# A recorded and re-ordered attention + FFN kernel: another transfer model and instruction pages in its planner, 10 warming matmuls for 20

## The chip, the cores and the metric

One core of a Trainium2 chip. The metric is device time of one execution in microseconds (us). Engines: PE (TensorE matmul), PEld (its weight loads), DVE (VectorE), ACT (ScalarE), SP (SyncE, which issues all the transfers here).

## The reference

```python
# attention: 4 batches, 8 heads, 512 local + 32 global tokens, head size 64
s_g  = scale * q_g @ k_all.T ; out_g = sm(s_g) @ v_all          # global queries see all keys
s_ll = where(|i - j| <= 32, scale * q_l @ k_l.T, -1e9)          # local queries: a band
s_l  = concat([scale * q_l @ k_g.T, s_ll]) ; out_l = sm(s_l) @ concat([v_g, v_l])
x    = concat([out_g, out_l])                                   # 2176 rows of 512
# first FFN, 1536 wide
g = x @ w_gate ; x = (g / (1 + exp(-g)) * (x @ w_val)) @ w_out
# second FFN, 2048 wide
h = x @ w_in ; out = (max(h, 0) + alpha * min(h, 0)) @ w_out2
```

All data is float32. The weights come as pairs of words of 64 bits that the kernel converts; products are made in three passes of high and low halves.

## The kernel before, in words

The kernel has two parts. The first part (attention of all batches, the first FFN of batches 0 to 2, and the preparation of the second FFN's weights) is not issued as the Python code runs: a `Planner` records each operation of PE, DVE, ACT and SP as an atom with its reads, writes and a cost (`record`, `price`). `flush` then asks `order` for a sequence and issues the operations in it; each engine works through its own list strictly in order. `order` simulates the four engines: each engine has a time at which it is free, an atom is ready when its predecessors are done, and of the atoms that are ready within `LOOK` (0.1 us) the one with the earliest due time is taken. Due times come from the recorded order of the matmuls. Transfers have one common time, `dma`, to which each adds bytes / `DMA`. All instructions of the recorded part carry line L272 in the profile. The second part (from `nc.flush()` on, L1199 and later lines) is issued as written.

The head of the recorded part is the attention of batch 0: four pairs of heads, u0 to u3. For each: `mm` (scores: 32 products of 128 columns, each two matmul records in the profile, so 64), `soft` (DVE mask and maximum, ACT exp), `t` (4 transposes and a copy `pt`), `pv` (64 records), `to` (4 transposes, then `xa` as high and low half). Ahead of it `heat(HEAT)` issues matmuls on a zero tile. Then `visit1` runs the first FFN: per block f of 128 hidden columns 12 matmuls for g, 12 for v, 12 for the output product, with `sg` (ACT), `t` (DVE), and `h` as high and low half (ACT, then DVE) between. The attention of the next batch and the weight conversion are spread between these blocks. A conversion: a load into a `dbl` or `yp` buffer, two ACT steps, three DVE steps (`raw`, `dbl`, `raw`), then split into high and low halves (`w`), and a store for the second use.

From the second batch on `w2_prepare` converts the second FFN's weights in the same way: load to `dbl`, convert, store `w2sx`, `w2so` from `dbl`, and for sums `w2ss` in two halves, one from `raw` and one from a scratch in the tail of `xa` (`out_to`, L869 to L882). `xa` holds x.T of a batch, high and low halves. At the change to the unrecorded part, `third` (L1182) lays four operands (t3, t1, b21, t4) over all of `xa`.

Of the kernel before, what the change touches and what calls it, by code (L numbers as in the profile page):

```python
# [10 lines left out]
F32 = mybir.dt.float32  # L11
# [13 lines left out]
N3 = 320  # L25
# [6 lines left out]
GWIN = (1, 4, 13, 15, 7, 10)  # L32
NG = len(GWIN)
P = dict(
    SLACK=60.0, LOOK=0.1, SWITCH=4.0, MARGIN=0.5, HEAT=20, ND=3, NR=3, LAG=6,
    wr0=0.75, wr2=0.5, wr3=0.75, wr4=0.6, wr5=0.2,
    ns1=33, ns2=34, ns3=32, g1=1.0, g2=1.1, g3=1.0,
    lo0=0.0, lo1=0.0, lo2=0.0, lo3=0.0, hi0=0.0, hi1=0.25, hi2=0.25, hi3=0.5,
# [13 lines left out]


class Op:
    __slots__ = ("eng", "op", "args", "kw", "reads", "writes", "cost", "lat", "table")


class Planner:
# [6 lines left out]


    ENGINES = ("tensor", "vector", "scalar", "sync")
    TABLE, DMA, START, LAST = 1.28, 405.0, 0.75, 10.0

    def __init__(self, tc):  # L70
        self.tc, self.nc = tc, tc.nc
# [51 lines left out]
    @staticmethod  # L123
    def price(o, outs, ins):
        n = int(np.prod(outs[0].shape[1:]))
        psum = any("PSUM" in str(a.space) for a in ins)
        o.lat = 0.14
        if o.eng == "tensor":
            o.lat = 0.23
            if o.op == "transpose":  # L130
                o.cost = n * 2 / 2400 + 0.003
            elif ins[0].dtype == F32R:
                o.cost = n / 2400 + 0.0133
            elif ins[0].dtype == BF16:
                o.cost = n / 2400 + 0.007
            elif n == 128:
                o.cost = 0.037
            else:
                o.cost = n * 4 / 2400 / 4 + 0.008
        elif o.eng == "vector":  # L140
            two = o.op in ("tensor_scalar", "tensor_copy") and not psum and ins[0].dtype == F32
            o.cost = n / (1920 if two else 960) + 0.075 + (n * 7 / 960 if o.op == "reciprocal" else 0)
        elif o.eng == "scalar":
            o.lat = 0.16
            wide = ins[0].ap[-1][0] > 1 or ins[0].dtype == U32
            o.cost = n / 1200 + 0.075 + (0.2 if o.kw.get("accum_out") is not None else 0) + (0.12 if wide else 0)
            f = o.kw.get("func")
            o.table = None if f == ACTF.Copy else f
        else:
            o.cost = 0.45  # L150
            a = outs[0]
            o.lat = int(np.prod(a.shape)) * mybir.dt.size(a.dtype) / 1e3 / Planner.DMA
# [27 lines left out]
    def order(self):  # L180
# [20 lines left out]
                d = min(d, due[j] - size[i] - atoms[i][-1].lat)  # L201
            due[i] = d
        free = {e: self.START for e in self.ENGINES}
        table, dma = None, 0.0
        left = [len(b) for b in before]
        done = [None] * N
        ready = {e: {} for e in self.ENGINES}
# [18 lines left out]
        while len(plan) < N:  # L226
# [19 lines left out]
            done[i] = []  # L246
            y = x
            if e == "sync":
                y += 0.45
                dma = max(dma, y + 1.0) + atoms[i][0].lat  # L250
                done[i] = [dma + 0.9]
            else:
                for o in atoms[i]:
                    y += o.cost
                    done[i].append(y + o.lat)
            free[e] = y
# [65 lines left out]
def kernel(  # L322
# [44 lines left out]

    ident = const.tile([128, 128], F32, name="ident")
    ex = Slots(const, {"y30": (1, 1024), "y31": (1, 1024)})
    xa = const.tile([128, 2, 4, 640], F32R, name="xa")  # L370
    yp = [const.tile([128, 2, 4, 256], F32, name=f"yp{b}") for b in range(B - 1)]
    y3 = {}

# [487 lines left out]
    def w2_prepare():  # L861
# [6 lines left out]
        def out_to(key, raw):  # L868
            w2s[key] = dram.tile([128, 2, 1024], F32, name="w2s%s%d" % key)  # L869
            if key[0] != "s" or not nc.recording:  # L870
                t = dbl.bitcast(F32R).rearrange("p (h c) -> p h c", h=2)
                yield from split(t, raw)
                nc.sync.dma_start(out=w2s[key], in_=t.bitcast(F32))
                return
            hi, lo = xa.rearrange("p h k c -> p (h k) c")[:, :, S:640], raw.rearrange("p (k c) -> p k c", c=128)
            st["tail"] = True
            nc.scalar.activation(out=hi, in_=lo, func=ACTF.Copy)
            yield
            nc.vector.tensor_tensor(out=lo.bitcast(F32R), in0=lo, in1=hi, op=ALU.subtract)
            nc.sync.dma_start(out=w2s[key][:, 0].rearrange("p (k c) -> p k c", c=128), in_=hi.bitcast(F32))  # L880
            nc.sync.dma_start(out=w2s[key][:, 1], in_=raw)
            st["tail"] = False  # L882

# [152 lines left out]
    if True:  # L1036
# [145 lines left out]
        def third():  # L1182

            while wq:
                wload(True)
            while st.get("tail"):
                next(w2gen)
            flat = xa.rearrange("p h k c -> p (h k c)")
            for i, name in enumerate(("t3", "t1", "b21", "t4")):
                ops1[name] = oper(flat[:, 4 * N3 * i:4 * N3 * i + 4 * N3], N3)  # L1190
            x_split(2, ops1["b11"], (0, 0))
            for name in ("t2", "t3", "t1"):
                x_split(2, ops1[name], sums[name])
            x_split(2, ops1["b21"], (1, 0))
            x_split(2, ops1["t4"], sums["t4"])
# [182 lines left out]
        x_split(0, ops["t1"], t1)  # L1378
        t4 = next(sums)[1]
        x_split(0, ops["t3"], next(sums)[1])  # L1380
        flat = xa.rearrange("p h k c -> p (h k c)")
        for i, name in enumerate(("b21", "t4", "b22")):
            ops[name] = oper(flat[:, 4 * NT * i:4 * NT * i + 4 * NT], NT)
        x_split(0, ops["b21"], (1, 0))
        x_split(0, ops["t4"], t4)
        x_split(0, ops["b22"], (1, 1))
# [194 lines left out]
```

## Time and profile before

| | |
|---|---|
| median of 3 runs | 897.06 us (897.03 to 897.11) |
| the profiled execution | 896.01 us |
| its span, first to last instruction | 894.2 us |
| mean granted clock of TensorE, as a share of full | 0.997 |
| PE busy | 866.7 us (97%) |
| DVE busy | 692.1 us (77%) |
| ACT busy | 528.2 us (59%) |

A row of a timeline gives the start in us, the time in us, engine, line, operation, output <- input with shapes, and the number of instructions merged; in brackets the engine's idle time before it and what ended it. "issue" stands for a wait for nothing that the profile shows. Matmul records overlap, since matmuls are pipelined. The tile a, g, v, acc stand for banks of PSUM.

### The profile page before, as it was taken

Reading aid. Unit: us, or ns where it says so; the run is one execution under the profiler, and the core shown is the slowest. Engines: PE = TensorE matmul, PEld = TensorE weight load, DVE = VectorE, ACT = ScalarE, POOL = GpSimd, SP = SyncE. Lnnn points to the kernel's source line nnn. Section 1 sums busy time; section 2 is a strip of 40 time slices with the busy share of each in tenths; the row PEclk is TensorE's granted clock in tenths of the full one; section 3 lists DMA queues with packets and bytes.
Section 4 is the critical chain, followed back from the end, with each engine's and each line's share of the span. In section 5 each row is a group of like instructions: output and inputs, shape, how many; then the busy total and the mean of one; then the engine's idle time right before and its main releaser. Section 6 shows DMA issues by size and latency. Waiting matters only on the chain.

```text
span 894.2 us, 17315 instructions
## 1 busy us (share of the span) xinstructions
PE 866.7 (97%) x6868; PEld 749.0 (84%) x6868; DVE 692.1 (77%) x1442; ACT 528.2 (59%) x1051; POOL 0.7 (0%) x6
## 2 busy tenths in 40 slices
PE   6799999999899999899999999999999999999997
PEld 5577778787688787778999999999999999989996
DVE  4997889969778865688666677777896777977776
ACT  5889999767667688554333346434555434554442
POOL 0000000000000000000000000000000000000000
PEclk9999999999999999999999999999999999999999
DMA  9899899798986789985656665546375554675731
GB/s 360 300 393 414 334 354 361 289 351 321 407 358 219 301 323 370 335 306 192 212 189 206 237 247 212 228 156 267 142 266 229 211 213 172 252 272 225 280 141 60
DMA packets 48833, 239.30 MB, mean 268 GB/s; under 512 B 4848, under 2 KB 13680, under 8 KB 26480
## 3 DMA queue, kind: packets, MB, share of 16 engines
q1 hardware_dynamic: 48752, 238.19, 70.8%
q8 instruction: 54, 0.88, 0.4%
q14 instruction: 27, 0.22, 0.1%
HBM read 183.38 MB, written 54.79 MB: 266 GB/s over the span
## 4 chain that ended last, share of the span: by engine, by line
PE 78%; DMA 10%; ACT 5%; DVE 5%; issue 1%; SPq 0%; ACTq 0%; DVEq 0%
PE ps_acc L1451 21%; PE ps_g L1239 9%; PE ps_v L1239 9%; PE ps_a L1239 8%; PE acc L272 8%; PE v L272 7%; PE g L272 7%; PE a L272 5%; PE ps_acc L1296 3%; DMA dbl<-in_w_dram 3%; DMA w2so<-dbl 2%; PE ps_a L1296 2%; DMA w2sx<-dbl 2%; DVE dbl L272 1%; DMA yp<-in_w_dram 1%
## 5 line engine op out<-in xcount | busy, mean ns | idle before, releaser
L1451 PE MATMUL ps_acc<-w,hring 128*128 128x512 f32 x816 | 194.2, 391 | 0.0
L1451 PEld LDWEIGHTS ps_acc<-w,hring 128*128 128x128 f32 x816 | 152.0, 188 | 30.1 <-ACT hring L1420 0.3
L272 PE MATMUL acc<-h,w 128*128 128x512 f32 x432 | 108.2, 399 | 3.1 <-ACT h L272 2.2
L272 PE MATMUL g<-xa,w 128*128 128x512 f32 x432 | 107.8, 398 | 2.5 <-ACT sg L272 1.6
L272 PE MATMUL v<-xa,w 128*128 128x512 f32 x432 | 107.1, 396 | 0.2 <-issue 0.2
L1415 ACT ACTIVATE r<-c 128x384 f32<-128x384 f32 (+1 forms) x96 | 47.8, 498 | 92.9 <-DVE c L1247 92.9
L272 PEld LDWEIGHTS acc<-h,w 128*128 128x128 f32 x432 | 81.0, 191 | 22.3 <-ACT h L272 2.5
L1456 DVE TENSOR_TENSOR oacc<-ps_acc,oacc 128x512 f32<-128x512 f32 x119 | 81.9, 691 | 22.2 <-PE ps_acc L1451 20.9
L272 PEld LDWEIGHTS g<-xa,w 128*128 128x128 f32 x432 | 78.9, 188 | 22.8 <-ACT sg L272 3.0
L272 PEld LDWEIGHTS v<-xa,w 128*128 128x128 f32 x432 | 79.3, 188 | 18.6 <-issue 1.8
L1420 ACT ACTIVATE hring<-g 128x384 fp32r<-128x384 f32 (+1 forms) x96 | 48.6, 506 | 55.9 <-DVE g L1417 55.6
L272 ACT ACTIVATE e<-e,mx 128x128 f32<-128x128 f32 (+1 forms) x136 | 57.2, 423 | 14.6 <-DVE mx L272 14.2
L1421 DVE TENSOR_TENSOR hring<-g,hring 128x384 fp32r<-128x384 f32 (+1 forms) x96 | 51.1, 532 | 18.9 <-ACT hring L1420 16.1
L1417 DVE SCALAR_TENSOR_TENSOR g<-g,nal,r 128x384 f32<-128x384 f32 (+1 forms) x96 | 56.8, 591 | 10.4 <-ACT g L1416 9.7
L272 ACT ACT_TABLE_LOAD x46 | 59.0, 1283 | 8.0 <-PE g L272 6.6
L1416 ACT ACTIVATE g<-c 128x384 f32<-128x384 f32 (+1 forms) x96 | 47.9, 499 | 13.9 <-DVE hring L1421 13.9
L1239 PE MATMUL ps_g<-xa,w 128*128 128x320 f32 (+1 forms) x288 | 53.3, 318 | 0.2
L1239 PE MATMUL ps_v<-xa,w 128*128 128x320 f32 (+1 forms) x288 | 53.2, 319 | 0.1
L1239 PE MATMUL ps_a<-w 128*128 128x384 f32 (+1 forms) x288 | 51.4, 326 | 0.0
L1239 PEld LDWEIGHTS ps_g<-xa,w 128*128 128x128 f32 x288 | 47.1, 188 | 1.9 <-ACT p L1255 0.4
L1239 PEld LDWEIGHTS ps_v<-xa,w 128*128 128x128 f32 x288 | 46.8, 188 | 1.6 <-DVE u L1263 0.4
L1239 PEld LDWEIGHTS ps_a<-w 128*128 128x128 f32 x288 | 47.9, 188 | 0.1
(211 smaller groups left out, 1397.7 us busy)
## 6 DMA issues: line engine op xcount, KB each, us to landing
dbl<-in_w_dram SPq DMA_DIRECT2D x28, 1024.0 KB, 8.0
w<-w2so SPq DMA_DIRECT2D x24, 1024.0 KB, 5.3
w<-w2sx SPq DMA_DIRECT2D x24, 1024.0 KB, 4.8
w<-w2ss SPq DMA_DIRECT2D x24, 1024.0 KB, 6.4
v<-in_v_dram SPq DMA_DIRECT2D x15, 1024.0 KB, 10.0
qk<-in_qk_dram SPq DMA_DIRECT2D x14, 688.0 KB, 9.5
w2sx<-dbl SPq DMA_DIRECT2D x8, 1024.0 KB, 8.0
w2so<-dbl SPq DMA_DIRECT2D x8, 1024.0 KB, 9.7
```

Of the source, the lines that this page charges most:

```text
L272: last[o.eng] = getattr(getattr(self.nc, o.eng), o.op)(*o.args, **o.kw)
L1239: nc.tensor.matmul(out=o[:, 0:n], lhsT=left(name, a, k), rhs=x[name][:, b, k, 0:n], start=(i == 0), stop=(i == 5),)
L1296: mm = nc.tensor.matmul(out=o, lhsT=a, rhs=x, start=(first and e == 0 and not second), stop=((j, f, e) == (NF1 // 2 - 1, 0, 2) and i not i ...
L1415: nc.scalar.activation(out=rr, in_=u, func=ACTF.Relu)
L1416: nc.scalar.activation(out=g, in_=u, func=ACTF.Relu, scale=-1.0)
L1417: nc.vector.scalar_tensor_tensor(out=g, in0=g, scalar=nal[:, i:i + 1], in1=rr, op0=ALU.mult, op1=ALU.add)
L1420: nc.scalar.activation(out=hi, in_=g, func=ACTF.Copy)
L1421: nc.vector.tensor_tensor(out=lo, in0=g, in1=hi, op=ALU.subtract)
L1451: nc.tensor.matmul(out=o, lhsT=a, rhs=x, start=(i == 0), stop=(i == 5))
L1456: nc.vector.tensor_tensor(out=oacc[tb], in0=o, in1=oacc[tb], op=ALU.add)
```

## The change

Four things. `HEAT` goes from 20 to 10. In the planner's simulation a transfer now starts 0.3 us after SP takes it up (before: 1.0 us after the 0.45 us of its issue), runs at 385 instead of 405 bytes per ns and is done 1.9 instead of 0.9 us after its last byte. PE's instructions are counted there (4 for a float32 matmul, 2 for others, 66 ahead of the first), and PE enters a page of 256 no sooner than 6.2 us after the page before. And `xa` becomes one flat tile: the first 4096 columns are x.T in rows of 512 (before: in rows of 640, of which the last 128 were the scratch), the last 1024 the scratch `tail`.

```diff
-    SLACK=60.0, LOOK=0.1, SWITCH=4.0, MARGIN=0.5, HEAT=20, ND=3, NR=3, LAG=6,
+    SLACK=60.0, LOOK=0.1, SWITCH=4.0, MARGIN=0.5, HEAT=10, ND=3, NR=3, LAG=6,
...
-    TABLE, DMA, START, LAST = 1.28, 405.0, 0.75, 10.0
+    TABLE, DMA, START, LAST, PAGE, FIRST, FETCH = 1.28, 385.0, 0.75, 10.0, 256, 66, 6.2
...
-        o.lat = 0.14
+        o.lat, o.words = 0.14, 0
         if o.eng == "tensor":
             o.lat = 0.23
+            o.words = 4 if o.op == "matmul" and ins[0].dtype == F32 else 2
...
-        table, dma = None, 0.0
+        table, dma, words, entered = None, 0.0, self.FIRST, [self.START]
...
             if e == "sync":
+                dma = max(dma, y + 0.3) + atoms[i][0].lat
+                done[i] = [dma + 1.9]
                 y += 0.45
-                dma = max(dma, y + 1.0) + atoms[i][0].lat
-                done[i] = [dma + 0.9]
             else:
                 for o in atoms[i]:
+                    words += o.words
+                    while words >= self.PAGE * len(entered):
+                        if len(entered) > 1:
+                            y = max(y, entered[-1] + self.FETCH)
+                        entered.append(y)
                     y += o.cost
                     done[i].append(y + o.lat)
...
-    xa = const.tile([128, 2, 4, 640], F32R, name="xa")
+    xall = const.tile([128, 16 * N3], F32R, name="xa")
+    xa = xall[:, 0:8 * S].rearrange("p (h k c) -> p h k c", h=2, k=4)
+    tail = xall[:, 8 * S:8 * S + 1024]
...
-            hi, lo = xa.rearrange("p h k c -> p (h k) c")[:, :, S:640], raw.rearrange("p (k c) -> p k c", c=128)
             st["tail"] = True
-            nc.scalar.activation(out=hi, in_=lo, func=ACTF.Copy)
+            nc.scalar.activation(out=tail, in_=raw, func=ACTF.Copy)
             yield
-            nc.vector.tensor_tensor(out=lo.bitcast(F32R), in0=lo, in1=hi, op=ALU.subtract)
-            nc.sync.dma_start(out=w2s[key][:, 0].rearrange("p (k c) -> p k c", c=128), in_=hi.bitcast(F32))
+            nc.vector.tensor_tensor(out=raw.bitcast(F32R), in0=raw, in1=tail, op=ALU.subtract)
+            nc.sync.dma_start(out=w2s[key][:, 0], in_=tail.bitcast(F32))
             nc.sync.dma_start(out=w2s[key][:, 1], in_=raw)
...
-                ops1[name] = oper(flat[:, 4 * N3 * i:4 * N3 * i + 4 * N3], N3)
+                ops1[name] = oper(xall[:, 4 * N3 * i:4 * N3 * i + 4 * N3], N3)
```

The last replacement stands in the same form once more, for the operands of the second FFN.

## Rows read from the trace of the kernel before

**Rows 1.** The page: busy time and instructions of each engine; the instruction queue.

```profile
PE 866.7 (97%) x6868; PEld 749.0 (84%) x6868; DVE 692.1 (77%) x1442; ACT 528.2 (59%) x1051; POOL 0.7 (0%) x6
...
q8 instruction: 54, 0.88, 0.4%
```

**Rows 2.** Busy time by stretch: length, engines, PEclk, DMA share, GB/s.

```profile
0.00:50.00 50.00, 36.16 (x698) 27.79 (x698) 33.81 (x112) 35.30 (x93) 0.70 (x6) 1.00 0.88 340
50.00:200.00 150.00, 149.00 (x1692) 118.24 (x1696) 129.24 (x298) 136.15 (x260) 0.00 (x0) 1.00 0.92 354
200.00:240.00 40.00, 35.04 (x304) 26.45 (x293) 36.94 (x80) 30.20 (x48) 0.00 (x0) 0.96 0.95 361
...
233.40:236.70 3.30, 3.30 (x8) 2.65 (x9) 3.27 (x6) 1.19 (x2) 0.00 (x0) 0.50 1.01 382
...
420.00:890.00 470.00, 469.39 (x2606) 433.77 (x2604) 360.32 (x688) 204.96 (x437) 0.00 (x0) 1.00 0.56 211
```

**Rows 3.** PE's smaller waits, 200 to 240 us: us in total, times, longest.

```profile
PE a L272 <- DVE o L272: 0.7, 1, 0.7
PE a L272 <- ACT yp L272: 0.7, 1, 0.7
```

**Rows 4.** Timeline of PE, 0 to 29 us.

```profile
0.99 2.32 PE L272 MATMUL g<-zero 128*128 128x128 bf16 x20 [0.99 <-DVE zero L272]
5.96 1.96 PE L272 MATMUL a<-qk 64*32 64x128 f32 x64 [2.65 <-DMA qk<-in_qk_dram]
...
14.16 1.10 PE L272 MATMUL a<-v,pt 128*32 128x64 f32 x63 [0.45 <-issue]
...
15.78 1.12 PE L272 MATMUL acc<-yp 64*32 64x128 f32 x61
20.09 0.41 PE L272 MATMUL acc<-yp 64*32 64x128 f32 x3 [3.19 <-issue]
20.43 0.66 PE L272 MATMUL acc<-ident,o 128*128 128x128 f32 x4
...
27.33 1.10 PE L272 MATMUL acc<-v,pt 128*32 128x64 f32 x64 [0.93 <-ACT pt L272]
```

**Rows 5.** Timelines of DVE and ACT: the softmax of u3 begins.

```profile
20.54 0.29 DVE L272 CUSTOM_DVE_ANT_0 e<-acc,lm 128x128 f32<-128x128 f32 x1 [4.21 <-PE acc L272]
...
21.77 0.40 ACT L272 ACTIVATE e<-e,mx 128x128 f32<-128x128 f32 x1 [3.12 <-DVE mx L272]
```

**Rows 6.** The chain that ended last, 0 to 60 us: start, us, what.

```profile
37.66 9.61 DMA yp<-in_w_dram
...
50.32 1.16 PE a L272 x64
```

**Rows 7.** Busy time by stretch, 28 to 32 us.

```profile
28.00:30.00 2.00, 1.57 (x96) 1.24 (x84) 1.92 (x3) 2.00 (x5) 0.00 (x0) 1.00 0.17 66
30.00:32.00 2.00, 0.92 (x12) 0.59 (x13) 2.00 (x3) 2.00 (x3) 0.00 (x0) 1.00 0.00 0
```

**Rows 8.** Timeline of all engines, 222 to 238 us.

```profile
222.24 3.04 PE L272 MATMUL v<-xa,w 128*128 128x512 f32 x12
...
224.06 1.13 ACT L272 ACTIVATE raw<-dbl 128x1024 f32<-128x1024 f32 x1 [1.31 <-DMA w2ss<-raw]
...
230.57 0.68 DVE L272 TENSOR_TENSOR t<-v,sg 128x512 f32<-128x512 f32 x1
...
231.97 0.50 PE L272 MATMUL acc<-h,w 128*128 128x512 f32 x1 [2.19 <-ACT h L272]
...
233.37 4.37 PE L272 MATMUL acc<-h,w 128*128 128x512 f32 x11 [0.91 <-DVE h L272]
...
234.76 6.93 SPq L272 DMA_DIRECT2D dbl<-in_w_dram  x1
```

**Rows 9.** Timeline of all engines, 367 to 373 us.

```profile
369.04 1.12 ACT L272 ACTIVATE raw<-dbl 128x1024 f32<-128x1024 f32 x1 [3.17 <-DMA dbl<-in_w_dram]
...
370.70 0.66 PE L272 MATMUL a<-ident,o 128*128 128x128 f32 x4 [2.49 <-ACT pt L272]
```

More of the change, by code (lines that the diff above doesn't have):

```diff
@@ L54 @@
 class Op:
-    __slots__ = ("eng", "op", "args", "kw", "reads", "writes", "cost", "lat", "table")
+    __slots__ = ("eng", "op", "args", "kw", "reads", "writes", "cost", "lat", "table", "words")
 class Planner:
     ENGINES = ("tensor", "vector", "scalar", "sync")
-    TABLE, DMA, START, LAST = 1.28, 405.0, 0.75, 10.0
+    TABLE, DMA, START, LAST, PAGE, FIRST, FETCH = 1.28, 385.0, 0.75, 10.0, 256, 66, 6.2
     def __init__(self, tc):
@@ L1187, in third @@
                 next(w2gen)
-            flat = xa.rearrange("p h k c -> p (h k c)")
             for i, name in enumerate(("t3", "t1", "b21", "t4")):
-                ops1[name] = oper(flat[:, 4 * N3 * i:4 * N3 * i + 4 * N3], N3)
+                ops1[name] = oper(xall[:, 4 * N3 * i:4 * N3 * i + 4 * N3], N3)
             x_split(2, ops1["b11"], (0, 0))
@@ L1380 @@
         x_split(0, ops["t3"], next(sums)[1])
-        flat = xa.rearrange("p h k c -> p (h k c)")
         for i, name in enumerate(("b21", "t4", "b22")):
-            ops[name] = oper(flat[:, 4 * NT * i:4 * NT * i + 4 * NT], NT)
+            ops[name] = oper(xall[:, 4 * NT * i:4 * NT * i + 4 * NT], NT)
         x_split(0, ops["b21"], (1, 0))
```

## Prediction

> **What bounds the kernel now.** I read the page first, then the stretches, then PE's own waits, then the timeline around each wait. The page says that PE is busy 97% of the span [rows 1], so a gain can only be a gap of PE. The stretches say where the gaps are: 0 to 50 us has 13.8 us without a matmul, 50 to 200 has 1.0, 200 to 240 has 5.0, and from 420 on, in the code that is not recorded, it is 0.6 us in 470 [rows 2]. The change touches the order of the recorded part alone, so 420 to 894 stays; what is to be had is some 20 us, of which the first 6 (until the first load is there) can't go.
>
> In the head the reader should look at one matmul block. The scores of the last pair (`u3.mm`) are 64 matmuls; 61 run from 15.78, then PE stands still 3.19 us with nothing to wait for ("issue"), and the last 3 run at 20.09 [rows 4]. Both other engines stand behind those 3: DVE is idle 4.21 us before the softmax of u3, ACT 3.12 us [rows 5]. I take this for the end of a page of instructions, by two counts. The instruction queue moved 54 pieces of 16 KB, 256 instructions of 64 bytes each; PE has 6868 matmuls and as many weight loads, 13,736, which is 53.7 x 256 [rows 1]. And 349 matmuls (20+64+64+8+64+64+4+61) run before the stall: 698 instructions and the 66 of `FIRST` make 764, four short of 3 x 256. The page before was entered at 14.16, after a smaller wait of the same kind [rows 4]: 5.9 us apart, near the `FETCH` of 6.2.
>
> In 200 to 240 PE waits for h: it stands 2.19 and 0.91 us and then runs 11 matmuls in 4.37 us where 12 take 3.04, since the granted clock fell to 0.50 after the pause, the lower of its two levels (1.2 GHz) [rows 2, 8]. The cause stands higher up in that timeline. The value matmuls that h needs started at 222.24, so their sum was there by 225.3; DVE does `t` only at 230.57, because ahead of it in its fixed order stand a weight conversion's steps, which wait for ACT, which waited until 224.06 for a store to land [rows 8]. The planner had thought that store sooner done. At 367 the same: ACT waits 3.17 us for a load, behind it stands a copy that PE waits 2.49 us for [rows 9].
>
> **The change part by part.** The sum is made against the profiled execution, 896.0 us (span 894.2 and 1.8 around it); the median of the runs is 897.06, 1.05 more.
>
> *HEAT 10 for 20.* Ten matmuls of 2 instructions go. They run at 0.99 to 3.31, and PE is then idle 2.65 us until the first load lands [rows 4]: their time costs and gives nothing. Their pace (2.32 us for 20 of 128 columns) is the lower clock's, so the 20 had not raised it before they ended; what raises it is the score blocks after them. But every page boundary moves 10 matmuls later. If the order stays, the 3 last matmuls of u3 then lie before the boundary, and the stall falls 7 matmuls behind them, in the transposes (the x4 at 20.43 and what follows) [rows 4]. u3's scores then end at 20.09 - 3.19 + 0.41 = 17.3, and DVE, idle since 20.54 - 4.21 = 16.33, begins at 17.3: 3.2 us sooner; ACT 3.1 [rows 4, 5]. Is that kept? From there DVE works almost without a gap (1.92 and 2.00 of 2 us [rows 7]) to the release of a load buffer, and the load issued at 37.66 (9.61 us to landing) lies on the chain to PE at 50.32 [rows 6]. The DMA engines have room to do it sooner: shares 0.17 and 0.00 in 28 to 32, 3.7 us idle [rows 7]. Against it: the page after the stall still comes at 20.1, the next not before 20.1 + 5.9 = 26.0, and that boundary lies inside the block that runs from 27.33 [rows 4], near 27.8: on PE's side only 1.8 us can be gained by then. Between 1.8 and 3.2 I take 2.5. Ends: 3.2, and a loss of 1.0 if the stall lands ahead of something that both engines want.
>
> The Trainium skill (Runtime: NRT & Kernel Launch, section Instruction fetch mechanics) says that refilling in blocks of 256 instructions is mostly hidden and that the issue floor hides it. By that rule the boundary costs nothing and moving it gives 0. The row of 3.19 us speaks against the rule.
>
> *Pages in the simulation.* They cost nothing on the chip; they only make the plan's PE time in the head later, as it is. From 50 us on, matmuls of 512 columns stand between the attention's and 128 matmuls take far longer than a fetch (1692 in 150 us, 11 us a page [rows 2]); there the term is idle. Value 0 beyond the 2.5.
>
> *DMA model.* For a lone 1 MB transfer, old: 1.45 + 2.59 + 0.9 = 4.94 us; new: 0.3 + 2.72 + 1.9 = 4.92. So nothing changes for a lone transfer. In a queue that doesn't run dry the new one lands 5% of the queued time later (2.5 us for 50 us) and 1.0 more at the end: some 3.5 us later. That is the size of the error that the two stalls show: DVE's `t` came 5 us late, ACT's copy 3. I take it that the new plan puts `t` and h ahead of the conversion: 2.19 + 0.91 and the slow matmuls (4.37 for 11 against 3.04 x 11/12 = 2.79, so 1.6) give 4.7; ends 0 and 6.1 (two smaller waits of that stretch, 1.4 [rows 3], too). For 367: 2.5 [rows 9]; ends 0 and 2.5. What is late next in both places is the conversion itself, whose product PE needs much later.
>
> The Trainium skill (DMA: Bandwidth & Descriptors, section Specifications) puts the ceiling of the fabric at 435 GB/s. By an estimate from that page 1 MB needs 2.4 us, the model of 405 would be nearer than that of 385, and the new plan would expect loads too late. The trace doesn't agree: over the long stretches, bytes by share give 340/0.88 = 386, 354/0.92 = 385 and 361/0.95 = 380 [rows 2]; the sum stays.
>
> *A new order makes new stalls.* The atoms of some 400 us are dealt out anew, on four in-order queues, SP's among them: a store that waits for its producer holds the loads behind it. What it will cost can't be read; its bounds are nothing and two stalls like the dearest one seen, 2 x 4.7. I take one, 4.7, since the old plan has one such and one of 2.5 in 370 us.
>
> *xa in one piece.* The scratch for the low halves was eight strips of 512 bytes a partition and is now one of 4096: eight stores of 1024 small packets become stores of 128. The load issued right behind one took 6.93 us to issue [rows 8], but the stretch's share of 0.95 [rows 2] says that the engines had work meanwhile: 0, ends 0 and -1.0. The operands t3, t1, b21, t4 now lie over other quarters of xa; t3 must wait three more matmuls of the last pass (0.7 us), and PE reads it some 7 us later: 0, and at most 0.7.
>
> Sum: -2.5 - 4.7 - 2.5 + 4.7 = -5.0; 896.0 - 5.0 = 891.0, as a median 892.1.
>
> **The rivals.** (a) *Only the head counts*: the plan after 50 us hardly changes, since a lone transfer costs the same; 897.06 - 2.5 = 894.6. For it: DVE and PE leave the planner little choice where both are full. Against: a share of 0.95 at 200 to 240 [rows 2], where the models differ. (b) *The stall doesn't move*: it is no page, or the new order puts another block on the boundary; the head gives 0, the rest -2.5 net: 894.6. The counts above speak against; a reordered head speaks for. The skill's rule on hidden fetches would end here. (c) *No new stall*: 897.06 - 9.7 = 887.4. (d) *The gain is swallowed*: the DMA share is 0.95 in 200 to 240, so work that comes earlier only queues longer there: 897. For it: a load into `dbl` waits for the store out of the same buffer, so the round of load, conversion and store has a length of its own. (e) *Slower: the h stall returns elsewhere.* The planner still ranks by due times that know nothing of how an in-order queue blocks; wherever a conversion's step whose load is later than simulated stands ahead of t or h, PE pauses and the clock falls, 4.7 us each. With the stall of 200 to 240 kept and two new ones, head -2.5 and 367 -2.5: 897.06 + 9.4 - 5.0 = 901.5. It decides from the second stall on, once the head and 367 are paid back. Against it: landings are now modelled later, which makes such steps rarer.
>
> **How the numbers follow.** Forecast 0.38, (a) 0.16, (b) 0.08, (c) 0.12, (d) 0.09, (e) 0.17. About 0.2%, 1.8 us, is what a measurement of this kernel can tell from no change: under 895.3 is faster, over 898.9 slower. Faster: 0.38 + 0.12 and 0.20 of the 0.24 of (a) and (b): 0.70. Same: (d) and the rest: 0.13. Slower: 0.17. The forecast's own range is 889 to 895. The range 886.0 to 900.0 takes in (c) and the nearer half of (e).
>
> **What would show it.** Right: the wait of kind "issue" in 16 to 20 us stands behind a complete block of 64 scores, DVE's softmax of u3 starts near 17.3, the block at 50.3 starts near 47.8; the granted clock doesn't fall at 233; the matmul stream from 420 on is the same, shifted. Wrong: the stall splits another score block; or a new pause of PE over 2 us with a fall of the clock in 100 to 400.

## The result and the profile after

The changed kernel takes 888.19 us (median of 4 runs, 885.66 to 890.1) where the kernel before took 897.04 beside it: ratio 0.990 (95% interval 0.988 to 0.993), 8.9 us or 1.0% faster. The forecast was 892.1. The profiled execution of after is the longest of its four, 890.1 us with a span of 888.3, against 896.0 and 894.2 before; from profile to profile the gain is 5.9 us, and the rest of the 8.9 lies in how the two executions stand to their medians.

The page of after, busy time and instructions of each engine, the packets of all transfers, and the instruction queue:

```profile
PE 866.2 (98%) x6858; PEld 748.8 (84%) x6858; DVE 690.1 (78%) x1442; ACT 527.5 (59%) x1051; POOL 0.7 (0%) x6
...
DMA packets 41665, 239.30 MB, mean 269 GB/s; under 512 B 4848, under 2 KB 5488, under 8 KB 19312
...
q8 instruction: 54, 0.88, 0.4%
```

PE's work is that of [rows 1] less ten matmuls; all the gain is in PE's gaps. The same stretches as in [rows 2], with the two in which the clock is low (columns: stretch, length, PE, PEld, DVE, ACT, POOL busy, granted clock, DMA share, GB/s):

```profile
0.00:50.00 50.00, 37.30 (x716) 27.61 (x721) 34.29 (x112) 36.31 (x94) 0.70 (x6) 0.97 0.91 346
50.00:200.00 150.00, 149.07 (x1701) 118.06 (x1681) 137.48 (x314) 138.15 (x261) 0.00 (x0) 1.00 0.95 367
200.00:240.00 40.00, 38.84 (x369) 30.78 (x366) 33.69 (x76) 33.64 (x56) 0.00 (x0) 1.00 1.01 399
240.00:420.00 180.00, 177.47 (x1532) 144.00 (x1531) 127.92 (x263) 116.47 (x211) 0.00 (x0) 0.99 0.79 291
...
23.30:26.60 3.30, 3.30 (x48) 2.25 (x36) 2.10 (x5) 3.30 (x16) 0.00 (x0) 0.50 1.02 411
...
313.40:316.80 3.40, 3.40 (x10) 2.62 (x9) 3.32 (x6) 2.52 (x8) 0.00 (x0) 0.50 0.50 142
```

200 to 240 went from 5.0 us without a matmul to 1.2, and the low clock of 233 is gone; it comes now at 23 and at 313. The head, PE's timeline:

```profile
0.99 1.25 PE L278 MATMUL g<-zero 128*128 128x128 bf16 x10 [0.99 <-DVE zero L278]
7.44 1.97 PE L278 MATMUL a<-qk 64*32 64x128 f32 x64 [5.20 <-DMA qk<-in_qk_dram]
...
17.03 1.16 PE L278 MATMUL acc<-yp 64*32 64x128 f32 x64
18.12 0.66 PE L278 MATMUL acc<-ident,o 128*128 128x128 f32 x4
18.61 0.49 PE L278 MATMUL acc<-ident,e 128*128 128x128 f32 x3
21.46 0.27 PE L278 MATMUL acc<-ident,e 128*128 128x128 f32 x1 [2.36 <-ACT e L278]
...
49.63 1.16 PE L278 MATMUL a<-qk 64*32 64x128 f32 x64 [0.93 <-ACT pt L278]
```

u3's scores are one block of 64 now, and the pause stands seven matmuls behind it, between the third and the fourth of the four transposes (before: after 61 of the 64 [rows 4]). DVE is idle only 0.42 us before the softmax of u3 (before: 4.21 [rows 5]):

```profile
18.24 0.29 DVE L278 CUSTOM_DVE_ANT_0 e<-acc,lm 128x128 f32<-128x128 f32 x1 [0.42 <-PE acc L278]
```

The first load landed 1.48 us later in this execution (7.44 for 5.96), so counted from there the softmax starts at 10.80 where it started at 14.58, and the block of [rows 6] (50.32 before, 49.63 after) at 42.19 where it started at 44.36. Next 219 to 229 (PE, ACT and DVE, to be read beside [rows 8]):

```profile
220.14 3.02 PE L278 MATMUL v<-xa,w 128*128 128x512 f32 x12
...
227.28 0.50 PE L278 MATMUL acc<-h,w 128*128 128x512 f32 x1
...
228.95 2.79 PE L278 MATMUL acc<-h,w 128*128 128x512 f32 x11 [1.17 <-DVE h L278]
...
219.59 1.16 ACT L278 ACTIVATE raw<-dbl 128x1024 f32<-128x1024 f32 x1
...
221.82 1.23 DVE L278 SCALAR_TENSOR_TENSOR dbl<-dbl 128x1024 int32<-128x1024 int32 x1 [0.34 <-ACT dbl L278]
...
225.81 0.68 DVE L278 TENSOR_TENSOR t<-v,sg 128x512 f32<-128x512 f32 x1
```

ACT's `raw` waits for no store any more, DVE's `t` starts at 225.81 for 230.57, PE waits 1.17 us in place of 2.19 and 0.91, and the 11 matmuls take 2.79 us at the full clock. The wait at 367 [rows 9] is gone as well: from 365.89 to 375.23 PE's blocks follow one another. In its place stands one new chain, at 304 to 317:

```profile
304.43 1.12 ACT L278 ACTIVATE raw<-dbl 128x1024 f32<-128x1024 f32 x1 [3.37 <-DMA w2ss<-raw]
...
307.24 1.23 DVE L278 SCALAR_TENSOR_TENSOR dbl<-dbl 128x1024 int32<-128x1024 int32 x1 [2.67 <-ACT dbl L278]
...
311.70 0.66 PE L278 MATMUL a<-ident,e 128*128 128x128 f32 x4 [2.25 <-DVE mx L278]
...
312.74 4.59 PE L278 MATMUL g<-xa,w 128*128 128x512 f32 x12
```

It is the old stall's pattern: ACT waits 3.37 us for a store, DVE 2.67 behind ACT, PE 2.25 for DVE, then 12 matmuls at the lower clock (0.50, which is 1.2 GHz) take 4.59 us for some 3.04.

All the stages can be set side by side by a count that no order changes: the start of the n-th (counted from 0) of the first FFN's 1296 matmuls of 512 columns in the recorded part, worked out from the trace of each kernel (us from the span's start). The names e1 to e12 are those of the experiments below.

| kernel | 1st load | 400th | 600th | 800th | 1000th | 1290th | end |
|---|---|---|---|---|---|---|---|
| before | 5.96 | 160.69 | 217.40 | 281.08 | 339.76 | 417.56 | 894.23 |
| after | 7.44 | 159.57 | 215.97 | 274.25 | 337.07 | 411.08 | 888.32 |
| after, profiled again (e8) | 5.93 | 158.86 | 215.35 | 273.63 | 334.03 | 408.03 | 885.21 |
| HEAT 10 alone (e1) | 6.10 | 158.86 | 214.51 | 278.84 | 337.52 | 413.00 | 889.83 |
| DMA model alone (e2) | 6.13 | 159.73 | 214.98 | 272.26 | 330.94 | 405.94 | 883.51 |
| xa alone (e3) | 5.66 | 162.10 | 218.92 | 283.61 | 342.29 | 416.68 | 893.34 |
| HEAT 10 and DMA model (e5) | 5.77 | 157.27 | 212.52 | 269.68 | 328.36 | 404.79 | 882.44 |
| after, pages free (e6) | 5.97 | 159.73 | 214.98 | 273.55 | 332.24 | 407.45 | 884.88 |
| after, old DMA model (e7) | 6.10 | 159.47 | 215.26 | 278.90 | 340.99 | 417.26 | 894.66 |
| after, HEAT 20 (e4) | 5.78 | 160.49 | 216.13 | 274.56 | 333.24 | 407.65 | 884.32 |
| HEAT 10, rate alone (e9) | 7.00 | 159.23 | 214.48 | 271.64 | 330.32 | 405.34 | 882.78 |
| HEAT 10, start and end (e10) | 5.61 | 159.98 | 217.42 | 280.59 | 339.27 | 416.49 | 893.30 |
| HEAT 0 and DMA model (e11) | 5.78 | 157.90 | 213.15 | 270.31 | 328.99 | 403.99 | 881.75 |
| HEAT 10, later landings (e12) | 5.83 | 159.16 | 214.80 | 271.96 | 330.64 | 405.49 | 887.37 |

From profile to profile: up to the 400th -1.1 (with a first load 1.5 later), to the 600th -0.3, to the 800th -5.4, to the 1000th +4.1, to the 1290th -3.8, behind that +0.6. The sum is -5.9. From the 800th to the 1000th every kernel takes 58.7 us but three: after (62.8), after profiled again (60.4) and after with the old DMA model (62.1), the three whose planner counts pages with HEAT 10.

### The profile page after: what moved, and what is told of

It is laid out like the page before. It is cut to its first block, busy times and chain, and to the rows that moved or that the text cites. A ratio compares the mean times of both kernels' runs of the same rounds, so it can differ in the third digit from the quotient of the medians.

```text
span 888.3 us, 17297 instructions
## 1 busy us (share of the span) xinstructions
PE 866.2 (98%) x6858; PEld 748.8 (84%) x6858; DVE 690.1 (78%) x1442; ACT 527.5 (59%) x1051; POOL 0.7 (0%) x6
## 4 chain that ended last, share of the span: by engine, by line
PE 68%; ACT 12%; DVE 11%; DMA 6%; issue 1%; SPq 0%; ACTq 0%; DVEq 0%
PE ps_acc L1456 21%; PE ps_g L1245 9%; PE ps_v L1245 9%; PE ps_a L1245 8%; PE g L278 5%; PE v L278 5%; PE acc L278 4%; ACT e L278 4%; PE ps_acc L1302 3%; DMA w2ss<-raw 2%; DVE raw L278 2%; PE a L278 2%; DVE dbl L278 2%; PE ps_a L1302 2%; ACT L278 2%; ACT dbl L278 2%
## 5 line engine op out<-in xcount | busy, mean ns | idle before, releaser
L278 PE MATMUL acc<-h,w 128*128 128x512 f32 x432 | 106.3, 395 | 1.2 <-DVE h L278 1.2
L1420 ACT ACTIVATE r<-c 128x384 f32<-128x384 f32 (+1 forms) x96 | 47.8, 498 | 93.1 <-DVE c L1253 93.1
```

The lines of the kernel that those rows point to most:

```text
L278: last[o.eng] = getattr(getattr(self.nc, o.eng), o.op)(*o.args, **o.kw)
L1420: nc.scalar.activation(out=rr, in_=u, func=ACTF.Relu)
```

## The experiments

Ratios are to the kernel before on the same chip, with 95% intervals. The kernel before had medians of 895.26 (e1 to e4), 893.97 (e5 to e8) and 895.18 us (e9 to e12) on the three chips used, and spread over some 5 us on each.

**HEAT alone.** The kernel before with one number changed:

```diff
-    SLACK=60.0, LOOK=0.1, SWITCH=4.0, MARGIN=0.5, HEAT=20, ND=3, NR=3, LAG=6,
+    SLACK=60.0, LOOK=0.1, SWITCH=4.0, MARGIN=0.5, HEAT=10, ND=3, NR=3, LAG=6,
```

> The kernel before with HEAT=10 and nothing else; every engine's order is the same, only ten matmuls of the warming are gone. If the stall of 3.19 us is the end of a page of 256 instructions (my theory), it moves ten matmuls later: the 64 score matmuls of u3 stand complete ahead of it, DVE's idle time before the softmax of u3 falls from 4.2 to under 1 us, and the time falls by 1 to 3 us, to 894 to 896; the pause at 229 to 237 us with the fall of the clock stays. If the stall is no page (rival), it stays behind 61 of the 64 and the time stays at 897.0 within 0.5. If the warming held the clock up (second rival), the first score blocks run slower and the time is over 897.5.

Measured 892.28 us, ratio 0.997 (0.995 to 0.998), 3.0 us. PE's timeline of this kernel, head and middle:

```profile
16.11 1.16 PE L272 MATMUL acc<-yp 64*32 64x128 f32 x64
...
17.69 0.49 PE L272 MATMUL acc<-ident,e 128*128 128x128 f32 x3
20.54 0.37 PE L272 MATMUL acc<-ident,e 128*128 128x128 f32 x1 [2.36 <-ACT e L272]
...
228.94 0.80 PE L272 MATMUL acc<-h,w 128*128 128x512 f32 x1 [2.19 <-ACT h L272]
230.34 5.06 PE L272 MATMUL acc<-h,w 128*128 128x512 f32 x11 [0.61 <-DVE h L272]
```

The pause moved by the ten matmuls, and the stall in the middle stayed, with 11 slow matmuls of 5.06 us where before has 4.37. DVE's softmax of u3 starts at 17.32 here, the block of [rows 6] at 48.49 (50.32 before). By the table the lead is 1.8 us at the 400th matmul. Compared instruction by instruction, every engine's order is that of before (only the ten matmuls are gone), so what else differs in the two profiles, above all that nothing waits at 367 here, is the executions' own.

**No warming matmuls at all**, with the new DMA model:

```diff
-    SLACK=60.0, LOOK=0.1, SWITCH=4.0, MARGIN=0.5, HEAT=20, ND=3, NR=3, LAG=6,
+    SLACK=60.0, LOOK=0.1, SWITCH=4.0, MARGIN=0.5, HEAT=0, ND=3, NR=3, LAG=6,
...
-    TABLE, DMA, START, LAST = 1.28, 405.0, 0.75, 10.0
+    TABLE, DMA, START, LAST = 1.28, 385.0, 0.75, 10.0
...
+                dma = max(dma, y + 0.3) + atoms[i][0].lat
+                done[i] = [dma + 1.9]
                 y += 0.45
-                dma = max(dma, y + 1.0) + atoms[i][0].lat
-                done[i] = [dma + 0.9]
```

> The kernel before with the new transfer model and HEAT=0: no warming at all, every page boundary 10 matmuls later than with HEAT=10. Theory (the warming does nothing but move the boundaries): the stall stands after 349 matmuls again, now 13 behind the transposes that follow u3's scores, the head is no slower than with HEAT=10, ratio 0.984 to 0.990. Rival (warming brings the clock up sooner): the first score blocks take longer, the head loses over 1 us, ratio 0.991 and more.

Measured 884.59 us, ratio 0.988 (0.985 to 0.990), the lowest ratio of all, though its interval overlaps with those of the DMA model alone (e2), with HEAT 10 (e5) and of the rate alone (e9). PE's timeline of it:

```profile
5.78 1.96 PE L272 MATMUL a<-qk 64*32 64x128 f32 x64 [5.78 <-DMA qk<-in_qk_dram]
...
17.49 1.16 PE L272 MATMUL acc<-yp 64*32 64x128 f32 x64
...
20.47 0.24 PE L272 MATMUL g<-v,pt 128*32 128x64 f32 x1
21.04 1.10 PE L272 MATMUL g<-v,pt 128*32 128x64 f32 x63 [0.32 <-issue]
...
27.23 0.69 PE L272 MATMUL acc<-v,pt 128*32 128x64 f32 x18 [1.10 <-issue]
```

The first 64 scores take 1.96 us with 0, 10 (1.97 in after) and 20 warming matmuls [rows 4], where the 64 scores of u3 take 1.16: warming doesn't make the first ones faster. And ten matmuls fewer move the boundary on again: now it lies behind the first of the 64 value products, and PE stands 0.32 us. The next pause of this kind, 1.10 us at 27.23, comes behind 477 matmuls, 128 matmuls of 2 instructions (256) and 6.2 us after the restart at 21.04. How long PE stands is not a matter of the place alone: in all fourteen profiles it goes on with the 350th matmul between 19.9 and 22.1 us, and the pause ahead of it (0.32 to 3.47 us) is shorter where PE comes there later.

**The DMA model alone**, in the kernel before (the last two changes of the diff above, with HEAT 20):

> The kernel before with the new transfer model in the simulation and nothing else (HEAT=20, no pages, old xa). My theory: the model alone moves h ahead of the conversion's steps: PE's waits in 200 to 240 us fall from 5.0 to under 2 us, the clock does not fall at 233, the stall at 367 goes, and the head with its 3.19 us stays; one new stall may come. Time 889 to 894. Rival (the gain of the changed kernel comes from the head, by HEAT and pages): 896 to 898, with the pause at 229 to 237 in its place.

Measured 885.66 us, ratio 0.989 (0.987 to 0.990): 9.6 us, as much as the whole change, and faster than the 889 to 894 that were expected. PE in the head, and the stretch of the h stall:

```profile
16.31 1.12 PE L272 MATMUL acc<-yp 64*32 64x128 f32 x61
20.90 0.41 PE L272 MATMUL acc<-yp 64*32 64x128 f32 x3 [3.47 <-issue]
...
200.00:240.00 40.00, 40.00 (x370) 31.52 (x370) 36.93 (x84) 30.48 (x52) 0.00 (x0) 1.00 0.96 375
```

With 20 warming matmuls the pause splits the 64 scores after 61, as before, though the plan is another. In 200 to 240 PE doesn't wait at all. From the 400th matmul to the 1290th this kernel takes 246.2 us where before takes 256.9.

**Which number of the DMA model.** HEAT 10 and the rate alone:

```diff
-    TABLE, DMA, START, LAST = 1.28, 405.0, 0.75, 10.0
+    TABLE, DMA, START, LAST = 1.28, 385.0, 0.75, 10.0
```

> The kernel before with HEAT=10 and of the new transfer model the rate alone: 385 instead of 405 bytes per ns, start and completion as before. PE and SP then stand in the same order as with the whole model, DVE and ACT in nearly the same. My theory: the 5% that add up in a queue that doesn't run dry are what the old model lacked, so the ratio is that of HEAT=10 with the whole model, 0.986 to 0.991. Rival (the 1.0 us more to completion is what counts): 0.995 to 0.998, as HEAT alone.

and HEAT 10 and the start and end of a transfer alone:

```diff
+                dma = max(dma, y + 0.3) + atoms[i][0].lat
+                done[i] = [dma + 1.9]
                 y += 0.45
-                dma = max(dma, y + 1.0) + atoms[i][0].lat
-                done[i] = [dma + 0.9]
```

> The kernel before with HEAT=10 and of the new transfer model the start (0.3 us) and the completion (1.9 us) alone, the rate stays at 405. Theory (the rate counts): the pause at 226 to 236 us with its fall of the clock is back, ratio 0.995 to 0.998. Rival (completion counts): 0.986 to 0.991 and no such pause.

Measured 885.63 us, ratio 0.990 (0.987 to 0.994), for the rate, and 893.26 us, 0.998 (0.996 to 0.999), for start and end: the second is no better than HEAT 10 alone. PE and DVE with the rate alone:

```profile
221.43 2.88 PE L272 MATMUL acc<-h,w 128*128 128x512 f32 x12
224.24 1.11 PE L272 MATMUL a<-qk 64*32 64x256 f32 x24
225.28 3.03 PE L272 MATMUL acc<-h,w 128*128 128x512 f32 x12
...
221.41 0.69 DVE L272 TENSOR_SCALAR raw<-raw 128x1024 f32<-128x1024 f32 x1
222.01 0.69 DVE L272 TENSOR_TENSOR t<-v,sg 128x512 f32<-128x512 f32 x1
222.61 1.22 DVE L272 SCALAR_TENSOR_TENSOR dbl<-dbl 128x1024 int32<-128x1024 int32 x1
```

PE with start and end alone:

```profile
231.49 0.51 PE L272 MATMUL acc<-h,w 128*128 128x512 f32 x1 [2.19 <-ACT h L272]
232.90 4.37 PE L272 MATMUL acc<-h,w 128*128 128x512 f32 x11 [0.90 <-DVE h L272]
```

At 385 the plan puts `t` between two steps of the conversion and the stall is gone; at 405 it is there with the old length, whatever start and end are. Start and end hardly touch the plan: PE's order is that of before, and on DVE 25 of the 743 instructions of the recorded part stand elsewhere. With the rate alone PE's and SP's orders are those of the whole model (PE in all but 4 places), and 71 of DVE's differ.

**Landings modelled later still.** HEAT 10 and the new DMA model with 4.0 for the 1.9:

```diff
-                done[i] = [dma + 1.9]
+                done[i] = [dma + 4.0]
```

> HEAT=10 and the new transfer model, but every transfer is simulated as done 4.0 us after its last byte instead of 1.9. Theory (what hurts is a landing later than simulated, so a pessimistic model is harmless): ratio 0.986 to 0.992, no fall of the clock between 100 and 400 us. Rival (the accuracy of the model is what pays): 0.994 and more, with new stalls.

Measured 890.40 us, ratio 0.994 (0.992 to 0.996). In 200 to 240 PE is busy 40.00 of 40 us, but at the change to the unrecorded part PE waits:

```profile
406.85 0.89 PE L1239 MATMUL ps_g<-w,w 128*128 128x320 f32 x5
411.07 1.29 PE L1239 MATMUL ps_v<-xa,w 128*128 128x320 f32 x6 [3.33 <-ACT p L1255]
```

So "later is safer" isn't so here: the ratio lies outside the 0.986 to 0.992 of that theory, and from the 1290th matmul to the end this kernel takes 481.9 us where HEAT 10 and the DMA model take 477.7. That the late plan puts work which the next part needs behind work that could have waited would explain it; no run here shows that.

**xa alone.** The changed kernel with HEAT 20, the old DMA model and FETCH 0, which leaves the flat `xa`:

```diff
-    SLACK=60.0, LOOK=0.1, SWITCH=4.0, MARGIN=0.5, HEAT=10, ND=3, NR=3, LAG=6,
+    SLACK=60.0, LOOK=0.1, SWITCH=4.0, MARGIN=0.5, HEAT=20, ND=3, NR=3, LAG=6,
...
-    TABLE, DMA, START, LAST, PAGE, FIRST, FETCH = 1.28, 385.0, 0.75, 10.0, 256, 66, 6.2
+    TABLE, DMA, START, LAST, PAGE, FIRST, FETCH = 1.28, 405.0, 0.75, 10.0, 256, 66, 0.0
...
-                dma = max(dma, y + 0.3) + atoms[i][0].lat
-                done[i] = [dma + 1.9]
                 y += 0.45
+                dma = max(dma, y + 1.0) + atoms[i][0].lat
+                done[i] = [dma + 0.9]
```

> The changed kernel with HEAT=20, the old transfer model and a fetch time of 0, so that of the change only the flat xa with its tail in one piece is left. My theory: 897.0 within 0.7, since no wait of PE named this store. Rival (fewer small packets relieve the queue): 1 to 3 us faster, 894 to 896, with the 200 to 240 us stretch better.

Measured 895.64 us, ratio 1.001 (0.999 to 1.003); the kernel before has 895.26 on this chip, so that the time lies among the rival's 894 to 896 says nothing for it. The page of after counts 7168 packets fewer than that of before (48,833), which is eight stores of 128 in place of eight of 1024; they were worth nothing that can be measured.

**Pages in the simulation.** The changed kernel with FETCH 0 (so that pages cost nothing in the plan), and the changed kernel once more beside it:

```diff
-    TABLE, DMA, START, LAST, PAGE, FIRST, FETCH = 1.28, 385.0, 0.75, 10.0, 256, 66, 6.2
+    TABLE, DMA, START, LAST, PAGE, FIRST, FETCH = 1.28, 385.0, 0.75, 10.0, 256, 66, 0.0
```

> The changed kernel with a fetch time of 0 in the simulation, so that the pages do nothing there. My theory after the first four runs: the page term itself does not pay; without it the ratio is that of HEAT and model together, 0.984 to 0.988. Rival (the page term is worth something in the head, where PE is late by it): worse than the changed kernel, 0.991 to 0.994.

> The changed kernel as it is, beside the others on one chip: ratio 0.990 within 0.003. If its runs spread by 4 us as they did, a second profile should show whether the stall at 309 us with its fall of the clock belongs to every execution (my theory: it does, the order is fixed) or to some (rival: it hangs on when a store lands, and a run without it has a clock of 1.0 and is 4 us shorter).

Measured 886.01 us, ratio 0.990 (0.987 to 0.993), between the two ranges that were expected, and 886.09 us, 0.990 (0.988 to 0.993). The pages bring nothing that can be measured, but they do make another plan: without them PE's and SP's orders are those of the DMA model alone, and with them 393 of DVE's 743 instructions stand elsewhere, 381 of these behind 50 us. The stall at 309 belongs to that plan: without pages no wait of PE between 50 and 420 us is over 0.7 us in this profile. In the second profile of the changed kernel, ACT's `raw` that waited 3.37 us for its store waits 0.75, and PE waits further on:

```profile
301.18 1.20 ACT L278 ACTIVATE raw<-dbl 128x1024 f32<-128x1024 f32 x1 [0.75 <-DMA w2ss<-raw]
...
319.80 1.22 ACT L278 ACTIVATE raw<-dbl 128x1024 f32<-128x1024 f32 x1 [3.58 <-DMA dbl<-in_w_dram]
...
324.83 0.66 PE L278 MATMUL a<-ident,e 128*128 128x128 f32 x4 [1.03 <-DVE mx L278]
```

The order of the instructions is that of the first profile, and the same `raw` begins 3.25 us sooner, 2.6 of them beyond the lead that the whole execution has by then: PE's wait for `mx` that was 2.25 us is 0.16. Another conversion, 18 us on, waits 3.58 us for a load instead, and PE 1.03 behind it, with no fall of the clock from 24 to 880 us. So the rival held: the stall of 2.25 us is a risk that this order carries, not a price that it pays each time.

**The changed kernel with the old DMA model, and with HEAT 20:**

```diff
-    TABLE, DMA, START, LAST, PAGE, FIRST, FETCH = 1.28, 385.0, 0.75, 10.0, 256, 66, 6.2
+    TABLE, DMA, START, LAST, PAGE, FIRST, FETCH = 1.28, 405.0, 0.75, 10.0, 256, 66, 6.2
...
-                dma = max(dma, y + 0.3) + atoms[i][0].lat
-                done[i] = [dma + 1.9]
                 y += 0.45
+                dma = max(dma, y + 1.0) + atoms[i][0].lat
+                done[i] = [dma + 0.9]
```

> The changed kernel with the old transfer model in the simulation: HEAT=10, pages and the flat xa are left. My theory: the pause at 226 to 236 us with the fall of the clock is back, and the ratio is that of HEAT alone, 0.995 to 0.998. Rival (pages and HEAT carry the gain): 0.989 to 0.992.

```diff
-    SLACK=60.0, LOOK=0.1, SWITCH=4.0, MARGIN=0.5, HEAT=10, ND=3, NR=3, LAG=6,
+    SLACK=60.0, LOOK=0.1, SWITCH=4.0, MARGIN=0.5, HEAT=20, ND=3, NR=3, LAG=6,
```

> The changed kernel with HEAT=20 again. My theory: the page boundary falls into the score block of u3 again, the head loses what it won, 1 to 3 us: 889 to 891.5, and the middle keeps its gain. Rival (the pages in the simulation let the order work around the boundary wherever it falls): 888.2 within 0.7.

Measured 895.81 us, ratio 1.002 (1.000 to 1.004), slower than either range expected, and 890.91 us, 0.995 (0.993 to 0.997), as expected. Without the new DMA model the h stall is back (PE's timeline of the first of the two):

```profile
228.64 0.50 PE L278 MATMUL acc<-h,w 128*128 128x512 f32 x1 [2.19 <-ACT h L278]
230.05 5.06 PE L278 MATMUL acc<-h,w 128*128 128x512 f32 x11 [0.91 <-DVE h L278]
```

and the head's gain, 1.2 us at the 400th matmul, is lost by the 1290th, which stands 0.3 us sooner than before's: between the 800th and the 1000th this order takes 62.1 us where HEAT 10 alone takes 58.7. The kernel with HEAT 20 is 5.2 us behind the DMA model alone; the two differ in pages and xa, and xa by itself is worth nothing in the old order. The pages make another plan here, too, so that is the likely cause, but no run separates the two at HEAT 20. Its profiled execution is the fastest of its six (886.1; the others 889.8 to 892.6), so where the loss lies can't be read from it and stays open.

**HEAT 10 and the DMA model together**, without pages and xa (the diff of the kernel without warming matmuls, with HEAT 10):

> The kernel before with HEAT=10 and the new transfer model, no pages and the old xa. If the two gains lie in different stretches and both are kept (my theory: head -3.0 from HEAT alone, middle -9.6 from the model alone), the ratio is 0.9966 x 0.9886 = 0.985, some 882 to 883 where the kernel before takes 895 to 897. If the lead of the head is swallowed by the queue of transfers in the middle (rival), it is the model's own 0.9886.

Measured 884.79 us, ratio 0.989 (0.986 to 0.992): by the medians the second alone, though with the intervals of all three the sum, 0.985, isn't ruled out. By the table its lead over the DMA model alone is 2.5 us at the 400th, 600th, 800th and 1000th matmul and 1.2 at the 1290th: between the last two it waits where the other doesn't. One of those waits is 0.99 us at 342 for ACT's `pt`. The order is the same but for 4 places on PE, and the kernel without warming matmuls, with that order too, leads by 1.8 us at the 400th matmul and still does at the end. So the traces keep a lead of 1 to 2 us, and whether the medians lose it isn't settled.

No version here is shown to beat the changed kernel: on its chip HEAT 10 and the DMA model have 884.79 beside 886.09, and the kernel without warming matmuls, on another chip, a ratio of 0.988 beside 0.990, with intervals that overlap.

## Why the prediction came out as it did

**Direction and the wide range (886.0 to 900.0) held; the forecast was 3.9 us too slow**, the forecast's own range, 889 to 895, was missed by 0.8 us, and the time lies nearer to rival (c), no new stall, 887.4, than to the forecast. That it came so near is in part luck. The two terms that could be run alone were worth more than the sum gave them (DMA model 9.6 us, HEAT 3.0: 12.6 together, and 9.7 in the sum), and the whole change keeps 8.9 of that, or 7.9 on the chip of e8. The 4.7 that was set aside for a new stall took the place of what is lost between the parts and the whole. Against the profiled execution the sum was 891.0 and 890.1 came; by terms:

| term | forecast | profile of after | what it is read from |
|---|---|---|---|
| head | -2.5 | -1.1, or -2.6 from the first load on | the 400th matmul |
| h stall of 200 to 240 | -4.7 | -5.4 | 600th to 800th |
| stall of 367 | -2.5 | -3.8 | 1000th to 1290th, with smaller waits |
| a new stall | +4.7 | +4.1 (e8: +1.7; none without pages) | 800th to 1000th |
| xa, pages | 0 | 0 | e3, e6 beside e8 |

**The head.** That the pause hangs on the count of instructions is shown: 349 matmuls run before it with HEAT 20, 10 and 0 alike, in old and new plans, and the next one, where PE stands at all, comes 128 matmuls on (e11: 1.10 us); which block it splits follows from the count alone. That it is the fetch itself the trace has too: it records the instruction queue's transfers of 16 KB one by one, and in all fourteen profiles PE goes on 1.25 to 1.51 us after the second of them has ended (before: it runs from 17.70 to 18.75, PE goes on at 20.09; after: 19.19 to 20.21, and 21.46). That DVE's softmax would begin near 17.3 came to 17.32 in HEAT 10 alone, and that kernel gained 3.0 us (1.5 to 4.7) where 2.5 was forecast, so rival (b) falls. Of the 3.2 us by which DVE starts sooner, 1.8 reach the 400th matmul, the lower of the two values between which 2.5 was taken; the block at 50.3, forecast near 47.8, started at 48.49 there, and at 49.63 and 48.97 in the two profiles of after. But the next boundary isn't what holds it to 1.8: no pause stands in the value products of after at 27.82, where the third transfer had ended at 26.09 and PE came to the boundary only at 28.31. And a part of the head that the sum didn't have is the clock: it is 0.50 in after from 23.3 to 26.6 and stayed at 1.00 in before [rows 2]; what that costs isn't separated. That the 20 warming matmuls ran at the lower clock is read from their pace alone: the profile's granted clock is 1.00 there. The Trainium skill (Runtime: NRT & Kernel Launch, section Instruction fetch mechanics) has the crossing of a block of 256 instructions as mostly hidden. That doesn't hold for this head: the pauses are 2.36 us in after and 3.47 in the DMA model alone, and only where PE comes late is it down to 0.32.

**The h stall.** That it would go was right, by the cause that was named: a plan that thinks transfers done too soon. How it goes was wrong in a part. In after the conversion's steps still stand ahead of `t` on DVE; they are 4.4 us sooner (1.4 of them since the whole kernel is, by the 600th matmul), and ACT's `raw` no longer waits for a store, and PE still waits 1.17 us. The first of these steps in before, beside the 221.82 of after:

```profile
226.25 1.23 DVE L272 SCALAR_TENSOR_TENSOR dbl<-dbl 128x1024 int32<-128x1024 int32 x1 [0.33 <-ACT dbl L272]
```

With the rate alone, in the old kernel, `t` stands between two of them, and PE's wait goes to nothing. What stood in the sum as two small changes (5% of the queued time, 1.0 us at the end) is in fact one: with HEAT 10 the rate takes the ratio from 0.997 to 0.990, and start and end leave it at 0.998. The Trainium skill (DMA: Bandwidth & Descriptors, section Specifications) has 435 GB/s as the fabric's ceiling. Of the two rates 405 lies nearer to that, and the runs speak for 385; bytes by share in after are 399/1.01 = 395 and 291/0.79 = 368 GB/s in the two long stretches from 200 to 420.

**The mis-sized term is the new stall.** As a mechanism it was right, with the same pattern and nearly its price in the profile (2.25 us of waiting, some 1.6 of slow matmuls). But it was entered as the price of any new order, and as if every execution paid it. The DMA model alone, a new order too, has no such stall (58.7 us from the 800th to the 1000th matmul, as before). It came with the pages, to which the sum gave nothing, since the term is idle behind the head; but a plan that differs in the head deals out anew what comes after. And it hangs on the landing of one store: e8 has 0.16 us there and 1.03 elsewhere, and the other runs of after lie 1.7 to 4.4 us under the profiled one; which of them had the stall isn't recorded. The same holds for the stall of 367. HEAT 10 alone has the order of before, and the kernel with `xa` alone has it but for four places each on DVE and ACT; in their executions the wait of [rows 9] is gone or short, with none of PE behind it (first HEAT 10, then `xa`):

```profile
364.18 1.12 ACT L272 ACTIVATE raw<-dbl 128x1024 f32<-128x1024 f32 x1
...
368.86 1.12 ACT L278 ACTIVATE raw<-dbl 128x1024 f32<-128x1024 f32 x1 [0.92 <-DMA dbl<-in_w_dram]
```

From the 1000th to the 1290th they take 75.5 and 74.4 us for 77.8, so the 2.5, too, were the price of one execution, and how much of the 3.8 in after is the new order's is open. Before's profile was 1.05 us under its median and after's 1.9 over, and 2.9 of the 3.9 us are these two; the other 0.9 is the sum itself.

**The rivals.** (a) falls with the DMA model alone, which has no head gain and 0.989. (d), a gain that is swallowed, is not what happened to the sum; inside it it may have happened in part, since by the medians head and DMA model together give no more than the DMA model, but the traces keep 1 to 2 us of the head's lead. (e), slower through stalls that return, is what pages and old DMA model do together (1.002 where HEAT 10 alone has 0.997) and what the later landings do at the handover (3.33 us); with the rate of 385 one such stall came, where (e) needed two and the old one kept.

**What would have shown it wrong**: a new pause of over 2 us with a fall of the clock in 100 to 400 was named, and came, at 309 to 313, in the profiled execution. That sign contradicts the sum, which counted one such stall in; it could only tell rival (c) from the forecast. Of the signs of being right the block at 50.3 came 0.7 us or more later than named, and the others came: u3's scores are one block, the clock doesn't fall at 233, and from the 1290th matmul on the time is that of before (477.2 for 476.7 us).

## What to carry to other kernels

In a planner that fixes an order by simulation the transfer rate counts: 5% in that one number was worth some 0.6% here (0.990 beside 0.997, with HEAT 10), because in-order queues turn a transfer that lands late into a wait of three engines and a low clock behind it; the rate is read from the long busy stretches of a trace, as bytes by share. Two rates were run, so that the measured one is the best isn't shown, and other plans with the same 385 came out at 0.994 and 0.995 (e12, e4): each change of the plan is a new deal. A pause of PE without a cause in the trace is to be counted, in instructions from the start: if it stands at the same count whatever the work there is, a few instructions more or fewer move it to where fewer engines wait behind it. And a stall that hangs on one landing is an execution's price, not the order's: two executions are to be compared before it goes into a sum.

## What the hardware showed

A page boundary is put down to different things in the trace: to "issue" in the DMA model alone (3.47 us), to "ACT e" in after and in HEAT 10 alone (2.36 us), and to "issue" again where the rate alone is changed, at the same place in the same transposes:

```profile
21.60 0.27 PE L272 MATMUL acc<-ident,e 128*128 128x128 f32 x1 [2.63 <-issue]
```

The place in the count tells it, not the name.

Each transfer of 256 instructions takes some 1.0 us in the head, the second starts 2.8 to 4.0 us after PE has begun the block before it (at the 222nd matmul), and PE goes on 1.25 to 1.51 us after it has ended: together the 5.9 us between 14.16 and 20.09 of before [rows 4].

In after the granted clock fell to 0.50 at 23, behind the pause of 2.36 us, and at 313, behind that of 2.25, and not at 229 behind 1.17. The length of the pause doesn't tell it alone: in before it stayed at 1.00 behind 3.19 us in the head [rows 2] and behind the 2.49 us at 370, while each of the other thirteen profiles has a stretch at 0.50 between 12 and 31 us. Before, 240 to 420 us, in the columns of [rows 2]:

```profile
240.00:420.00 180.00, 177.14 (x1588) 142.80 (x1587) 131.31 (x268) 121.57 (x217) 0.00 (x0) 1.00 0.83 305
```

Where it fell in a full stretch, the pause cost some 1.6 us more than itself in before and after, and over the 11 matmuls alone 2.3 us in HEAT 10 alone and in after with the old DMA model (5.06 for 2.79).

Warming matmuls on a zero tile, with a load to wait for behind them, didn't make the first scores faster: PE was idle 2.65 us behind 20 of them [rows 4], 5.20 behind 10 and 5.78 with none, and the first 64 scores took 1.96, 1.97 and 1.96 us.

The kernel before gave medians from 893.97 to 897.04 us in its four sets of runs beside other kernels, and on each of the three chips of the experiments runs some 5 us apart; so it is the ratios on one chip that are compared.
